# The last 64 weight rows: one load that names its source twice, in place of two half loads

## The chip, the cores and the metric

The kernel runs on one core of one Trainium2 chip. The core has TensorE (PE: matrix products; PEld: its weight loads), VectorE (DVE), ScalarE (ACT), GpSimd (POOL) and SyncE (SP, which issues DMAs and computes nothing), and 16 DMA engines that move data between HBM, the chip's main memory, and SBUF, the working memory of 128 partitions. The metric is the device time of the program in microseconds (us). For the kernel before, three runs gave 153.39 to 153.58 us with a median of 153.56 us.

## The reference

An input of 2048 tokens of width 448 is normalised over its width. The result feeds two branches, and both are added to the input:

```
xn  = layernorm(x)                                   # x: 2048 x 448
q, k, v = split(xn @ wqkv)                           # 16 heads of 28
phi(a)  = concat(softmax(a @ w_phi), softmax(-a @ w_phi))     # per head
num = phi(q) @ (phi(k)^T @ v);  den = phi(q) @ sum_s phi(k) + 1e-6
A   = (num / den) @ wo
B   = mish(xn @ w1 + b1) @ w2                        # 1792 hidden columns
out = x + A + B
```

Everything is bf16 in memory; the products are accumulated in 32 bits.

## The kernel before

**Tiles.** The 2048 tokens are 16 tiles of 128; two tiles make a unit u (8 units). The width of 448 is three chunks of 128 rows and one of 64. To use the full height of 128 rows of TensorE for the chunk of 64, the two tiles of a unit are put together: their normalised rows are transposed into seven chunks, three of each tile and one (chunk 3) whose upper half belongs to the first tile and whose lower half to the second. A product with a weight W is then run in passes: A and B cover the three full chunks in halves of 64 rows, two half products side by side, and H covers chunk 3. For H, both partition halves need the last 64 rows of W. That is why the last 64 rows (384 to 447) of the key and value weights and of W1 lie twice in SBUF: at chunk 3, in partitions 0 to 63 and again in 64 to 127.

**Loads.** A weight is loaded by two functions. `load_main` (line 275) brings rows 0 to 383 as three chunks. `load_tail` (line 279) brings the last 64 rows into both halves, with one DMA per half. It is called for the key and value weights together (`lkts`: rows of 896 numbers, 1792 bytes) and for W1 (`l1ts`: rows of 1792 numbers, 3584 bytes). Both calls are issued from SyncE.

**Order.** Each engine has one instruction stream. The streams are written out by one list of steps, ORDER (line 147); a step appends its instructions to the engines that it uses, so each engine executes its part of the list in that order. Waits between engines follow from named resources: each operation lists what it reads and writes, and `resolve` (line 89) turns this into waits on semaphores. A wait holds everything behind it on its engine.

The steps around the two tail loads, on the queues that matter:

- SyncE: x tiles 0 (`lx0.1s`), key weights (`lkms`), key and value tail (`lkts`), x tiles 8 and 9, b1, four transposing loads of the query weights (`lqT`), the transpose of unit 1 (`xt1m`), x tiles 10 and 11, W1's tail (`l1ts`), the transposes of units 3, 6, 4, 7 and 5 (`xt3m` and so on, DMA transposes at line 516), W1's main part (`l1ms`), and then transposes of the query features (line 690).
- ScalarE issues the other x tiles, w_phi in four small loads of 28 rows each (line 299), and the value weights' main part.
- TensorE at the start: 12 warm-up products of zeros (line 370), the transposes of the key weights in two halves `wtk0` and `wtk1` (line 547; the second half reads chunk 3, so it waits for the tail), the transpose of unit 0, the products of the transposed key weights with w_phi (`wmk0`, `wmk1`, line 571), the transpose of unit 2, and then key, value and query products (line 429), the first of which needs all of the folded key weights `Wpk`.
- VectorE and ScalarE take the results out of PSUM, TensorE's result memory (lines 509 and 511).

W1 is read first by `f0.0B`, the first product of the second branch. The first products that read the transposed units 3 and 6 are `k3B` and `v6Ba`.

`load_x` loads of two tiles have 128 rows of 1792 bytes, those of one tile 128 rows of 896 bytes.

Of the kernel before, what the change touches and what calls it, by code (L numbers as in the profile page):

```python
# [5 lines left out]
ACT = mybir.ActivationFunctionType  # L6
ALU = mybir.AluOpType
AX = mybir.AxisListType
FP32 = mybir.dt.float32
# [3 lines left out]
D = 448  # L13
H = 16
DH = 28
F = 1792
P = 128
# [9 lines left out]
QP = 56  # L27
# [11 lines left out]
class Program:  # L39
# [13 lines left out]
    def op(self, eng, fn, r=(), w=(), dma=False, tag="", after=()):  # L53
        o = Op()
        o.tag, o.parts = tag, None
        o.eng, o.fn, o.dma, o.needed, o.count, o.sem = eng, fn, dma, False, 0, None
        o.idx = len(self.ops[eng])
        deps = list(after)
        for res in list(r) + list(w):
            if res[0] == "ps":  # L60
                deps += [a for e, a in self.psum.get(res, {}).items() if e != eng]
        for res in r:
            if res[0] != "ps":
                deps += self.writers.get(res, [])
        for res in w:
            if res[0] != "ps":
                deps += [d for d in self.writers.get(res, []) if d.dma or dma or d.eng != eng]
                deps += [d for d in self.readers.get(res, []) if d.dma or dma or d.eng != eng]
        for res in r:
            if res[0] == "ps":  # L70
                self.psum.setdefault(res, {})[eng] = o
            else:
                self.readers.setdefault(res, []).append(o)
        for res in w:
            if res[0] == "ps":
                self.psum.setdefault(res, {})[eng] = o
            else:
                self.writers[res] = [o]
                self.readers[res] = []
        o.deps = deps  # L80
        self.ops[eng].append(o)
        self.order = getattr(self, "order", [])
        self.order.append(o)
        return o

    def dma(self, eng, fn, r=(), w=(), tag=""):
        return self.op(eng, fn, r, w, dma=True, tag=tag)
# [84 lines left out]
def _kernel(es, nc, A_x, A_wqkv, A_w_phi, A_wo, B_w1, B_b1, B_w2, out):  # L172
    def sb(name, shape, dtype):
        return es.enter_context(nc.sbuf_tensor(name, shape, dtype))
# [4 lines left out]
    ident = sb("ident", [P, P], BF16)  # L179
# [4 lines left out]
    x_all = sb("x_all", [P, NT, D], BF16)  # L184
    stats = sb("stats", [P, NT, 6], FP32)
    mv = sb("mv", [P, NT, 2], FP32)
    eps_col = sb("eps_col", [P, 1], FP32)
    mhalf = sb("mhalf", [P, 4], FP32)
    lnv = sb("lnv", [P, NT], FP32)
    rstd = sb("rstd", [P, NT], FP32)  # L190
    shift = sb("shift", [P, NT], FP32)
    NXN = 4
    xn = [sb(f"xn{i}", [P, 2 * D], BF16) for i in range(NXN)]
    xnT = sb("xnT", [P, NU, 7, P], BF16)
# [4 lines left out]
    Wkv = sb("Wkv", [P, 4, 2 * D], BF16)  # L199
    Wk, Wv = Wkv[:, :, 0:D], Wkv[:, :, D:2 * D]  # L200
    WqT = sb("WqT", [P, G, 4 * P], BF16)
    Wp = [sb(n, [P, 4, D], BF16) for n in ("Wpq", "Wpk")]
# [8 lines left out]
    v_all = v_flat[:, :].rearrange("p (u i h c) -> p u i h c", u=NU, i=2, h=H)  # L211
    EqT = sb("EqT", [P, NT, 2 * G, P], BF16)
# [14 lines left out]
    def act_flat(q):  # L227
        return actT[:, q, :, :].rearrange("p f n -> p (f n)")

    def E_of(u):  # L230
        return act_flat(1)[:, u * 4 * D:(u + 1) * 4 * D].rearrange("p (s i d) -> p s i d", s=2, i=2)
# [6 lines left out]
    def Eq_of(u):  # L238
        src = Eq0[:, :] if u % 3 == 0 else act_flat(0)[:, EQ_ROWS[u % 3] * 1024:(EQ_ROWS[u % 3] + 2) * 1024]
        return src.rearrange("p (i s c) -> p i s c", i=2, s=2)  # L240
# [2 lines left out]
    home_rows = {"Wk": [("Wk", 0), ("Wt", 0), ("Wt", 1)], "Wv": [("Wv", 0)], "Wq": [("WqT", g) for g in range(G)] + [("WqTd",)],  # L243
                 "Wp1": [("Wp", 1, h, c) for h in range(2) for c in range(2)]}

    def oT_of(u):
        t, at, _ = oT_home[u // 2]
        flat = t[:, :, :].rearrange("p c f -> p (c f)")
        return flat[:, at + (u % 2) * 7 * P:at + (u % 2 + 1) * 7 * P]
# [3 lines left out]
    def bank(b, n=1):  # L253
        return PS[:, b * TCW:(b + n) * TCW]

    def bank16(b):
        return PS.bitcast(BF16)[:, 2 * b * TCW:2 * (b + 1) * TCW]
# [5 lines left out]
    op, dma = pg.op, pg.dma  # L263

    def pb(b):
        return ("ps", b)

    HALF = ((0, 64), (64, 128))
# [8 lines left out]
            w=[(name, 0)], tag="ld" + name)  # L277

    def load_tail(eng, name, dst, src):
        for i, (lo, hi) in enumerate(HALF):  # L280
            dma(eng, lambda e, lo=lo, hi=hi: e.dma_start(dst[lo:hi, 3, :], src[384:448, :]),
                w=[("Wt", i) if name == "Wkv" else (name, 1 + i)], tag="ld" + name)

    def load_qT(g, eng):
        dma(eng, lambda e: e.dma_start_transpose(WqT[:, g, 0:D], A_wqkv[:, g * GP:g * GP + P]), w=[("WqT", g)],
# [6 lines left out]
    def rows_of(name):  # L292
        return [(name, 0), ("Wt", 0), ("Wt", 1)] if name in ("Wk", "Wv") else [(name, i) for i in range(3)]
# [87 lines left out]
    def touch(*banks):  # L381
        clock[0] += 1
        for b in banks:
            used[b] = clock[0]

    def take2(hold=True):
        free = [b for b in (0, 2, 4, 6) if b not in held]
        assert free, "no pair of banks"
        b = min(free, key=lambda b: max(used[b], used[b + 1]))
        touch(b, b + 1)  # L390
        if hold:
            held.add(b)
        return b

    def free2(b):
        held.discard(b)
        touch(b, b + 1)

    def take1():
        b = min((b for b in range(8) if b - b % 2 not in held), key=lambda b: used[b])  # L400
        touch(b)
        return b

    def pe(fn, r, w, tag, after=()):
        return op("PE", fn, r=r, w=w, tag=tag, after=after)
# [8 lines left out]
    def passes(part):  # L414
        if part == "F":
            return [(c, par, (0, P)) for par in range(2) for c in range(3)]
        x = int(part == "B")
        return [(c, r ^ x, HALF[r]) for c in ((3,) if part == "H" else range(3)) for r in range(2)]

    def pe_pass(fn, r, b, part, tag):  # L420
        o = pe(fn, r, [pb(b), pb(b + 1)], tag, after=[side[b, "A" if part == "B" else "B"]] if part in "ABH" and
               (b, "A" if part == "B" else "B") in side else [])
        side[b, "B" if part == "B" else "A"] = o

    def run(e, todo, works, first, last):
        at = {par: [n for n, x in enumerate(todo) if x[1] == par] for par in range(2)}
        for n, (c, par, k) in enumerate(todo):
            o, lhs, rhs = works[par]
            ins = e.matmul(o, lhs(c, k), rhs(c, k), start=first and n == at[par][0], stop=last and n == at[par][-1])  # L429
        return ins  # L430

    def pair_part(key, part, works, r, then):
        todo = passes(part)
        if key not in open_:
            open_[key] = [take2(), set()]
        b, done = open_[key]
        first = not done
        done.add(part)
        last = done in ({"F", "H"}, {"A", "B", "H"})
        pe_pass(lambda e: run(e, todo, works(b), first, last), r, b, part, key + part)  # L440
        if last:
            then(b)
            free2(b)
# [57 lines left out]
    def transpose7(e, b, src, cut=7):  # L501
        for c in range(7):
            to = bank16(b)[:, c * P:(c + 1) * P] if c < cut else bank16(b + 1)[:, (c - cut) * P:(c - cut + 1) * P]
            ins = e.transpose(to, src[:, c * P:(c + 1) * P], ident[:])
        return ins

    def evac(eng, dst, src, r, w, tag):
        if eng == "ACT":
            op("ACT", lambda e: e.activation(dst(), src(), ACT.Copy), r=r, w=w, tag=tag)  # L509
        else:  # L510
            op("DVE", lambda e: e.tensor_copy(dst(), src()), r=r, w=w, tag=tag)  # L511
# [80 lines left out]
    def xchunk(c, par):  # L592
        return c if c == 3 or par == 0 else 4 + c

    def tok_works(u, W):
        return lambda b: [(bank(b + par)[:, 0:D],
                           lambda c, k, par=par: xnT[k[0]:k[1], u, xchunk(c, par), :],
                           lambda c, k: W[k[0]:k[1], c, :]) for par in range(2)]

    def v_mm(u, part, eng):  # L600
        def then(b):
# [86 lines left out]
    def q_turn(t):  # L688
        u = t // 2
        dma("SP", lambda e: e.dma_start_transpose(EqT[:, t, :, :], Eq_of(u)[:, t % 2, :, :].rearrange("p s c -> p (s c)")),  # L690
            r=[("Eq", u % 3, 0), ("Eq", u % 3, 1)], w=[("EqT", t)], tag=f"eT{t}")

    def bias_T():
        b = take1()
# [169 lines left out]
    def add(name, fn, *args):  # L864
        steps[name] = lambda: fn(*args)
# [34 lines left out]
    for q in range(2):  # L900
        for part in "FABH":
            for fc in range(FC):
                add(f"f{q}.{fc}{part}", ffn1, q, fc, part)
    add("kvz", kvz)
    add("wob", last_weights)
    add("table", table)
# [73 lines left out]
```

## Time and profile before

| | us |
|---|---|
| median of three runs (lowest to highest) | 153.56 (153.39 to 153.58) |
| the profiled execution's own time | 153.96 |
| its span, first to last instruction | 152.2 |
| TensorE busy | 144.6 (95%) |
| VectorE busy | 101.1 (66%) |
| ScalarE busy | 75.7 (50%) |
| GpSimd busy | 44.3 (29%) |

The profile is of one execution. An engine's busy time is the time in which it executes something; a TensorE that is busy is not at its peak, since products overlap. "SPq" and "ACTq" mark DMA issues, which aren't counted as busy. The chain of waits is followed back from the last instruction, at each step to what released it. For a DMA issue the profile gives the size and the time from issue to landing. q1 is the queue of the DMAs that SyncE issues, q10 that of ScalarE's.

### The profile page before, as it was taken

The numbers are of one execution on the slowest core, as the hardware profiler recorded it, in microseconds if no ns is written. First come the engines' busy times: TensorE is split into PE (matmuls) and PEld (weight loads), VectorE is DVE, ScalarE is ACT, GpSimd is POOL, SyncE is SP. The second block draws the span as 40 slices with busy tenths as digits, with TensorE's granted clock in tenths as the row PEclk, the third lists the DMA queues.
The fourth block names the chain that finished last, engine by engine and source line by source line (L and its number), as shares of the span: only waits on it lengthen the run. The fifth ranks groups of instructions, "written<-read, shape, count | busy, mean of one in ns | idle before, by whom it ended". The sixth has DMA issues, their size and how long they took to land.

```text
span 152.2 us, 3611 instructions
## 1 busy us (share of the span) xinstructions
PE 144.6 (95%) x1541; PEld 76.1 (50%) x1541; DVE 101.1 (66%) x223; ACT 75.7 (50%) x90; POOL 44.3 (29%) x65
## 2 busy tenths in 40 slices
PE   3978999989999979999999999999999999999993
PEld 1454545445444574445344455554544554559552
DVE  0699989599969903599606999535995999200721
ACT  3485999995995699778997730000500400000000
POOL 3385688969999950000000000000000000000000
PEclk9999999999999999999999999999999999999999
DMA  5995964989967243994399260500035000540204
GB/s 123 288 260 147 174 143 93 131 268 262 101 137 138 76 139 73 180 197 41 60 149 321 86 65 14 119 0 0 2 65 151 30 4 0 121 121 4 87 4 151
DMA packets 40436, 17.22 MB, mean 113 GB/s; under 512 B 34020, under 2 KB 39908, under 8 KB 40420
## 3 DMA queue, kind: packets, MB, share of 16 engines
q1 hardware_dynamic: 37548, 14.46, 46.9%
q10 hardware_dynamic: 2872, 2.53, 5.6%
q8 instruction: 12, 0.20, 0.5%
q14 instruction: 4, 0.03, 0.1%
HBM read 7.02 MB, written 1.84 MB: 58 GB/s over the span
## 4 chain that ended last, share of the span: by engine, by line
PE 78%; ACT 12%; DMA 4%; DVE 3%; issue 1%; ACTq 0%
PE PS L429 38%; PE PS L828 28%; PE PS L845 7%; DMA x_all<-in_A_x_dram 4%; ACT actT L609 3%; PE PS L723 2%; PE PS L650 2%; ACT actT L682 2%; ACT v_all L509 2%; DVE Sk L627 1%; ACT Wpq L509 1%; ACT Eq L682 1%; DVE v_all L511 1%; ACT Eq L509 1%; ACT Wpk L509 1%
## 5 line engine op out<-in xcount | busy, mean ns | idle before, releaser
L703 ACT ACTIVATE actT<-PS,b1T 128x1024 bf16<-128x1024 f32 x28 | 30.2, 1112 | 33.1 <-PE PS L429 33.0
L429 PE MATMUL PS<-xnT,W 64*128 64x512 bf16 x392 | 46.2, 376 | 0.0
L828 PE MATMUL PS<-W,actT 128*128 128x448 bf16 (+1 forms) x224 | 42.7, 351 | 0.0
L828 PEld LDWEIGHTS PS<-W,actT 128*128 128x128 bf16 x224 | 21.5, 98 | 20.3 <-issue 0.7
L429 PEld LDWEIGHTS PS<-xnT,W 64*128 64x128 bf16 x392 | 18.1, 94 | 21.0 <-ACT actT L703 0.4
L793 DVE TENSOR_TENSOR x_all<-PS,x_all 128x448 bf16<-128x448 f32 (+1 forms) x16 | 9.5, 616 | 20.3 <-PE PS L845 10.3
L621 POOL TENSOR_TENSOR actT<-actT,rSk 128x896 bf16<-128x896 bf16 x12 | 20.0, 1699 | 0.0
L609 ACT ACTIVATE actT<-PS 128x896 bf16<-128x896 f32 x16 | 13.7, 950 | 3.7 <-DVE stats L466 1.8
L429 PE MATMUL PS<-Wkv,xnT 64*128 64x448 bf16 x112 | 13.6, 349 | 0.6 <-DVE v_all L511 0.6
L429 PE MATMUL PS<-Wpk,xnT 64*128 64x448 bf16 x112 | 13.3, 349 | 0.5 <-ACT Wpk L509 0.5
L429 PE MATMUL PS<-Wpq,xnT 64*128 64x448 bf16 x112 | 12.7, 350 | 0.0
L466 DVE BATCH_NORM_STATS2 stats<-x_all 128x6 f32<-128x448 bf16 x15 | 9.2, 614 | 5.2 <-DMA x_all<-in_A_x_dram 5.2
L617 DVE TENSOR_REDUCE Sk<-actT 128x32 f32<-128x896 bf16 x12 | 12.5, 1043 | 0.0
L738 DVE COPY Sq<-PS 128x16 f32<-128x16 f32 x32 | 4.0, 167 | 12.5 <-PE PS L723 12.2
L749 DVE TENSOR_TENSOR xn<-v_all,rden 128x448 bf16<-128x448 f32 x16 | 10.0, 625 | 1.3 <-DMA Wkv<-xn 0.8
L746 DVE TENSOR_TENSOR v_all<-v_all 128x464 f32<-128x464 f32 x16 | 10.3, 642 | 0.6
L742 DVE TENSOR_TENSOR v_all<-PS,Sq 128x464 f32<-128x464 f32 x16 | 10.3, 642 | 0.5
L744 DVE TENSOR_TENSOR v_all<-PS,Sq 128x464 f32<-128x464 f32 x16 | 10.1, 630 | 0.0
L429 PEld LDWEIGHTS PS<-Wkv,xnT 64*128 64x128 bf16 x112 | 5.4, 94 | 6.0 <-DVE v_all L511 1.0
L682 ACT ACTIVATE actT<-PS 128x896 bf16<-128x896 f32 x10 | 8.4, 926 | 0.0
L429 PEld LDWEIGHTS PS<-Wpk,xnT 64*128 64x128 bf16 x112 | 5.3, 94 | 5.5 <-ACT Wpk L509 0.6
L429 PEld LDWEIGHTS PS<-Wpq,xnT 64*128 64x128 bf16 x112 | 5.1, 94 | 5.4 <-ACT actT L609 0.5
(85 smaller groups left out, 137.7 us busy)
## 6 DMA issues: line engine op xcount, KB each, us to landing
W<-in_B_w_dram SPq DMA_DIRECT2D x1, 1568.0 KB, 8.0
out_dram<-x_all SPq DMA_DIRECT2D x7, 224.0 KB, 2.2
W<-in_B_w_dram SPq DMA_DIRECT2D x1, 1344.0 KB, 7.2
x_all<-in_A_x_dram ACTq DMA_DIRECT2D x5, 224.0 KB, 4.1
Wo<-in_A_wo_dram ACTq DMA_DIRECT2D x2, 336.0 KB, 3.6
x_all<-in_A_x_dram SPq DMA_DIRECT2D x2, 224.0 KB, 4.9
W<-in_B_w_dram SPq DMA_DIRECT2D x2, 224.0 KB, 4.0
Wkv<-in_A_wqkv_dram SPq DMA_DIRECT2D x1, 336.0 KB, 4.2
```

The lines of the kernel that those rows point to most:

```text
L429: ins = e.matmul(o, lhs(c, k), rhs(c, k), start=first and n == at[par][0], stop=last and n == at[par][-1])
L609: op("ACT", lambda e, s=s: e.activation(E_of(u)[:, s, :, :], two(b, D), ACT.Exp, scale=1.0 if s == 0 else -1.0), r=[pb(b), pb(b + 1)], w=[ ...
L617: op("DVE", lambda e: e.tensor_reduce(Sk[u][:, s, :], Eh(), AX.X, ALU.add), r=[("E", u, s)], w=[("Sk", u, s)], tag=f"Sk{u}.{s}")
L621: op("POOL", lambda e: e.tensor_tensor(Eh(), Eh(), ap_on(rSk[u][:, s, 0:1], [[1, 2 * H], [0, DH]]), ALU.mult), r=[("E", u, s), ("rSk", u, ...
L682: op("ACT", lambda e, s=s: e.activation(Eq_of(u)[:, :, s, :].rearrange("p i (h n) -> p i h n", n=64)[:, :, :, 0:QP], two(b, D).rearrange(" ...
L703: op("ACT", lambda e: e.activation(actT[:, q, fc, :], bank(b, 2), ACT.Mish, bias=b1T[:, fc:fc + 1]), r=[("b1T",), pb(b), pb(b + 1)], w=[(" ...
L742: op("DVE", lambda e: e.tensor_tensor(tv(t1[i]), num(0), sx(1), ALU.mult), r=[pb(b), pb(b + 1), ("Sq", i, 1)], w=[("t1", i)], tag=f"ta{t}")
L744: op("DVE", lambda e: e.tensor_tensor(tv(t2), num(1), sx(0), ALU.mult), r=[pb(b), pb(b + 1), ("Sq", i, 0)], w=[("t2",)], tag=f"tb{t}")
L746: op("DVE", lambda e: e.tensor_tensor(t1[i], t1[i], t2, ALU.add), r=[("t1", i), ("t2",)], w=[("t1", i)], tag=f"tc{t}")
L749: op("DVE", lambda e: e.tensor_tensor(o_sb[(t // 2) % 2][:, t % 2, :].rearrange("p (h d) -> p h d", d=DH), t1[i][:, :, 0:DH], ap_on(rden[i ...
L828: ins = e.matmul(bank(b)[:, 0:width(t)], act_of(fc, t), W2[:, fc, 0:width(t)], start=first and fc == 0, stop=last and fc == FC - 1)
L845: ins = e.matmul(bank(b)[:, 0:w], oT_of(u)[lo:hi, cc * P:(cc + 1) * P], Wo[lo:hi, cc, 0:w], start=first and n == at[par][0], stop=last and ...
```

## The change

The tail is loaded by one DMA. Its source is an access pattern with a leading dimension of count 2 and step 0, so that the 64 rows are named twice; its destination is chunk 3 in all 128 partitions. The resources written are the same two names, now by one DMA.

```diff
     def load_tail(eng, name, dst, src):
-        for i, (lo, hi) in enumerate(HALF):
-            dma(eng, lambda e, lo=lo, hi=hi: e.dma_start(dst[lo:hi, 3, :], src[384:448, :]),
-                w=[("Wt", i) if name == "Wkv" else (name, 1 + i)], tag="ld" + name)
+        rows = src[384:448, :]
+        twice = bass.AP(tensor=rows.tensor, offset=rows.offset, ap=[[0, 2]] + [list(d) for d in rows.ap])
+        dma(eng, lambda e: e.dma_start(dst[:, 3, :], twice), w=[("Wt", i) if name == "Wkv" else (name, 1 + i) for i in range(2)],
+            tag="lt" + name)
```

The diff also brings a small buffer, some new steps, and additional written names on the transposes of the query features. ORDER is unchanged, and it contains none of the new steps:

```diff
+    nrstd = sb("nrstd", [P, 8], FP32)
...
+    XR, XC = (15, 14, 13, 12), (11, 10, 9, 8)
...
+    def early_of(t):
+        return [(n, XR.index(t)) for n in ("xR", "xRU")] if t in XR else \
+            [("xc", XC.index(t), i, n) for i in range(2) for n in range(2 if i else 1)] if t in XC else []
...
     def q_turn(t):
...
-            r=[("Eq", u % 3, 0), ("Eq", u % 3, 1)], w=[("EqT", t)], tag=f"eT{t}")
+            r=[("Eq", u % 3, 0), ("Eq", u % 3, 1)], w=[("EqT", t)] + early_of(t), tag=f"eT{t}")
...
+    for u in range(4):
+        add(f"nr{u}", minus_rstd, u)
+        for eng, c in (("ACT", "a"), ("DVE", "d"), ("both", "b")):
+            add(f"ct{u}{c}", center_T, u, eng)
...
```

More of the change, by code (lines that the diff above doesn't have):

```diff
@@ L244, in _kernel, with flat_of, xR @@
                  "Wp1": [("Wp", 1, h, c) for h in range(2) for c in range(2)]}
+    XR, XC = (15, 14, 13, 12), (11, 10, 9, 8)
+    def flat_of(t):
+        return EqT[:, t, :, :].rearrange("p c n -> p (c n)")[:, 0:7 * P]
+    def xR(u):
+        return flat_of(XR[u]).rearrange("p (c n) -> p c n", n=P)
+    def early_of(t):
+        return [(n, XR.index(t)) for n in ("xR", "xRU")] if t in XR else \
+            [("xc", XC.index(t), i, n) for i in range(2) for n in range(2 if i else 1)] if t in XC else []
     def oT_of(u):
@@ L593, in xchunk, with tok_works, x_of, x_res @@
         return c if c == 3 or par == 0 else 4 + c
-    def tok_works(u, W):
-        return lambda b: [(bank(b + par)[:, 0:D],
-                           lambda c, k, par=par: xnT[k[0]:k[1], u, xchunk(c, par), :],
+    def tok_works(u, W, early=False):
+        def x_of(c, k, par):
+            return xR(u)[k[0]:k[1], xchunk(c, par), :] if early else xnT[k[0]:k[1], u, xchunk(c, par), :]
+        return lambda b: [(bank(b + par)[:, 0:D], lambda c, k, par=par: x_of(c, k, par),
                            lambda c, k: W[k[0]:k[1], c, :]) for par in range(2)]
+    def x_res(u, early):
+        return [("xR", u), ("xRU", u)] if early else [("xnT", u), ("xnU", u)]
@@ new lines, in center, with center_T @@
+    def center(t, eng):
+        u = t // 2
+        for n, (lo, hi, at) in enumerate([(0, D, 0)] if t % 2 == 0 else [(384, D, D), (0, 384, D + 64)]):
+            src, dst = x_all[:, t, lo:hi], flat_of(XC[u])[:, at:at + hi - lo]
+            op(eng, lambda e, src=src, dst=dst: e.tensor_scalar(dst, src, mv[:, t, 0:1], 0.0, op0=ALU.subtract, op1=ALU.add),
+               r=[("x", t), ("mean", t)], w=[("xc", u, t % 2, n), ("EqT", XC[u])], tag=f"xc{t}.{n}")
+    def center_T(u, eng):
+        r = [("xc", u, 0, 0), ("xc", u, 1, 0), ("xc", u, 1, 1), ("ident",)]
+        home = [("EqT", XR[u])]
+        if eng == "both":
+            b = take2(False)
+            pe(lambda e: transpose7(e, b, flat_of(XC[u]), 3), r, [pb(b), pb(b + 1)], f"cT{u}")
+            evac("ACT", lambda: xR(u)[:, 0:3, :].rearrange("p c n -> p (c n)"), lambda: bank16(b)[:, 0:3 * P], [pb(b)],
+                 [("xR", u)] + home, f"cTe{u}")
+            evac("DVE", lambda: xR(u)[:, 3:7, :].rearrange("p c n -> p (c n)"), lambda: bank16(b + 1)[:, 0:4 * P],
+                 [pb(b + 1)], [("xRU", u)] + home, f"cTf{u}")
+            return
+        b = take1()
+        pe(lambda e: transpose7(e, b, flat_of(XC[u])), r, [pb(b)], f"cT{u}")
+        evac(eng, lambda: flat_of(XR[u]), lambda: bank16(b)[:, 0:7 * P], [pb(b)], [("xR", u), ("xRU", u)] + home, f"cTE{u}")
@@ new lines, in minus_rstd, with sign_rstd, v_early, then @@
+    def minus_rstd(u):
+        op("DVE", lambda e: e.tensor_scalar(nrstd[:, 2 * u:2 * u + 2], rstd[:, 2 * u:2 * u + 2], -1.0, 0.0, op0=ALU.mult, op1=ALU.add),
+           r=[("rstd", 2 * u), ("rstd", 2 * u + 1)], w=[("nr", u)], tag=f"nr{u}")
+    def sign_rstd(t, s):
+        return nrstd[:, t:t + 1] if s else rstd[:, t:t + 1]
+    def v_early(u, part, eng):
+        def then(b):
+            for i in range(2):
+                t = 2 * u + i
+                dst, src = v_all[:, u, i, :, 0:DH], bank(b + i)[:, 0:D].rearrange("p (h d) -> p h d", d=DH)
+                r, w = [pb(b + i), ("rstd", t)], [("v", u)] if i else [("vh", u)]
+                if eng == "ACT":
+                    op("ACT", lambda e, dst=dst, src=src, t=t: e.mul(dst, src, rstd[:, t:t + 1]), r=r, w=w, tag=f"vs{u}.{i}")
+                else:
+                    op("DVE", lambda e, dst=dst, src=src, t=t: e.tensor_scalar(dst, src, rstd[:, t:t + 1], 0.0, op0=ALU.mult,
+                                                                               op1=ALU.add), r=r, w=w, tag=f"vs{u}.{i}")
+        pair_part(f"v{u}", part, tok_works(u, Wv, True), x_res(u, True) + rows_of("Wv"), then)
@@ new lines, in k_early, with then @@
+    def k_early(u, part):
+        def then(b):
+            for s in range(2):
+                for i in range(2):
+                    t = 2 * u + i
+                    op("ACT", lambda e, s=s, i=i, t=t: e.activation(E_of(u)[:, s, i, :], bank(b + i)[:, 0:D], ACT.Exp,
+                                                                    scale=sign_rstd(t, s)),
+                       r=[pb(b + i), ("rstd", t), ("nr", u)], w=[("E", u, s)] if i else [("Eh", u, s)], tag=f"exkc{u}.{s}.{i}")
+        pair_part(f"k{u}", part, tok_works(u, Wp[1], True),
+                  x_res(u, True) + [("Wp", 1, h, c) for h in range(2) for c in range(2)], then)
@@ new lines, in q_early, with then @@
+    def q_early(u, part):
+        def then(b):
+            for s in range(2):
+                for i in range(2):
+                    t = 2 * u + i
+                    op("ACT", lambda e, s=s, i=i, t=t: e.activation(
+                        Eq_of(u)[:, i, s, :].rearrange("p (h n) -> p h n", n=64)[:, :, 0:QP],
+                        bank(b + i)[:, 0:D].rearrange("p (h n) -> p h n", n=QP), ACT.Exp, scale=sign_rstd(t, s)),
+                       r=[pb(b + i), ("Eqp", u % 3), ("rstd", t), ("nr", u)], w=[("Eq", u % 3, s)],
+                       tag=f"exqc{u}.{s}.{i}")
+        pair_part(f"q{u}", part, tok_works(u, Wp[0], True), x_res(u, True) + [("Wp", 0, c) for c in range(4)], then)
@@ L903, in _kernel @@
                 add(f"f{q}.{fc}{part}", ffn1, q, fc, part)
+    for u in range(4):
+        add(f"nr{u}", minus_rstd, u)
+        for eng, c in (("ACT", "a"), ("DVE", "d"), ("both", "b")):
+            add(f"ct{u}{c}", center_T, u, eng)
+        for part in "ABH":
+            add(f"v{u}{part}e", v_early, u, part, "ACT")
+            add(f"v{u}{part}f", v_early, u, part, "DVE")
+            add(f"k{u}{part}c", k_early, u, part)
+            add(f"q{u}{part}c", q_early, u, part)
+        for t in (2 * u, 2 * u + 1):
+            add(f"xc{t}d", center, t, "DVE")
+            add(f"xc{t}p", center, t, "POOL")
     add("kvz", kvz)
```

## The prediction

> **What bounds the kernel now.** I read the page first (its span), then the chain of waits that ended last.
>
> ```profile
> span 152.2 us, 3611 instructions
> ```
>
> Chain of waits, in order of time (start, length, what):
>
> ```profile
> 1.74 5.48 DMA x_all<-in_A_x_dram
> ...
> 11.06 0.81 ACT Wpk L509
> ...
> 11.92 4.17 PE PS L429 x42
> ...
> 26.52 1.62 ACT Eq L682 x2
> ...
> 34.21 18.73 PE PS L429 x184
> ```
>
> The chain has no hole. Until 11.92 us it is the preparation of the key weights, until 34 us TensorE and ScalarE take turns, and from 34.21 us it is TensorE alone in long runs. So whatever holds TensorE before 34 us is paid at the end nearly in full, unless the work behind it had been waiting anyway. No tail load stands in the chain; they are hidden. The question is what covers them, and by how much. SyncE's queue:
>
> ```profile
> 1.27 0.42 SPq L276 DMA_DIRECT2D Wkv<-in_A_wqkv_dram  x1
> 1.74 1.19 SPq L281 DMA_DIRECT2D Wkv<-in_A_wqkv_dram  x2
> ...
> 16.49 1.11 SPq L281 DMA_DIRECT2D W<-in_B_w_dram  x2
> 18.98 9.90 SPq L516 DMA_TRANSPOSE xnT<-xn  x5
> ```
>
> **What the change removes.** One issue on SyncE per tail: 1.19/2 = 0.6 us at 1.7 us and 1.11/2 = 0.55 us at 16.5 us. SyncE is on the chain at neither place, so I price this at nothing; the cover is the x tiles on ScalarE's queue, which the chain waits for until 7.23 us. The new names and steps besides (nrstd, the early steps, the extra written names on the transposes of tiles 8 to 15) issue nothing in this order and meet no other reader or writer: nothing, but for 32 bytes per partition that move later buffers. Bytes stay the same: 64 rows, each landing twice.
>
> **What it adds: over how many DMA engines the load is spread.** The page has 16 of them. Does a load always use all? ScalarE's queue answers, because all its issues are listed:
>
> ```profile
> q10 hardware_dynamic: 2872, 2.53, 5.6%
> ...
> x_all<-in_A_x_dram ACTq DMA_DIRECT2D x5, 224.0 KB, 4.1
> Wo<-in_A_wo_dram ACTq DMA_DIRECT2D x2, 336.0 KB, 3.6
> ...
> Wkv<-in_A_wqkv_dram ACTq DMA_DIRECT2D x1, 336.0 KB, 3.8
> ...
> x_all<-in_A_x_dram ACTq DMA_DIRECT2D x1, 112.0 KB, 2.8
> Wo<-in_A_wo_dram ACTq DMA_DIRECT2D x2, 56.0 KB, 4.7
> ...
> out_dram<-x_all ACTq DMA_DIRECT2D x1, 96.0 KB, 1.7
> Wbd<-in_A_w_phi_dram ACTq DMA_DIRECT2D x4, 6.1 KB
> ```
>
> One packet per contiguous row: 6 x loads and one store of 128, three loads of 384, two of 64 make 2176; the four Wbd loads (28 rows of 4 pieces) make 448. Sixteen issues with sixteen reports of completion each would add 256: 2880. The page has 2872, eight fewer: two for each of the 28-row loads. So these report 14 times, not 16 (and are the ones with no time to landing). A load is dealt out by its leading count: 128 and 64 rows go to 16 engines, 28 rows to 14, the largest number up to 16 that divides 28. The new load has leading count 2 at its source (the name written twice) and 128 at its destination. The trace shows no such load; its bounds are 16 engines, if the destination's count decides, and 2, if both lists must divide. I take 2: a share must be cut at the same place in both lists, and the source list can be cut only into two.
>
> By the Trainium skill, page "DMA: Bandwidth & Descriptors", section "Rules for kernel authors", an outermost zero-step count c confines a DMA to at most c engines; the 14 reports agree with its counting rule, and the trace of before has no load with c = 2. The same section advises one 128-partition load over two half loads, which by itself would make the sum zero.
>
> **Price of two engines.** Rate of one engine, from stretches with full queues (length, then busy of PE, PEld, DVE, ACT, POOL, clock, DMA share, GB/s):
>
> ```profile
> 13.20:13.80 0.60, 0.60 (x10) 0.29 (x6) 0.60 (x3) 0.00 (x0) 0.52 (x2) 1.00 1.01 385
> 5.00:7.50 2.50, 2.50 (x13) 1.06 (x11) 1.24 (x4) 1.63 (x5) 1.20 (x3) 1.00 1.14 256
> 31.00:35.00 4.00, 3.40 (x38) 1.75 (x36) 3.97 (x4) 2.91 (x4) 2.84 (x3) 1.00 0.97 319
> ```
>
> 385/16 = 24 GB/s alone; 256/1.14/16 = 14 in the crowded start; 319/0.97/16 = 20.6 under large rows.
>
> *Key/value tail.* Each engine gets 64 x 1792 B = 114,688 B: 4.8 us at 24 GB/s, 8.2 us at 14. Landing times from issue: the load ahead (L276), then the two tails (L281):
>
> ```profile
> DMA to landing us min/median/max: 4.2/4.2/4.2
> ```
>
> ```profile
> DMA to landing us min/median/max: 5.2/5.2/5.3
> ```
>
> So before, the second half landed at 2.3 + 5.3 = 7.6 us. Now the tail begins when the load ahead is through, 1.3 + 4.2 = 5.5 us, and lands at 10.3 us if nothing shares its engines, at 13.7 us at the crowded rate. ScalarE's queue shares them:
>
> ```profile
> 6.36 0.40 ACTq L276 DMA_DIRECT2D Wkv<-in_A_wqkv_dram  x1
> 6.79 0.61 ACTq L273 DMA_DIRECT2D x_all<-in_A_x_dram  x1
> ```
>
> 336 + 224 KB over 16 engines at 24 GB/s are 1.5 us. I take T = 10.3 + 1.5 = 11.8 us. Who waits: the step wtk1, the second half of the L547 transposes, and behind it everything on TensorE, which runs in order.
>
> ```profile
> 7.17 1.17 PE L547 MATMUL PS<-ident,Wkv 128*112 128x128 bf16 x16
> ...
> 9.44 0.66 DVE L511 COPY Eq<-PS 112x1024 bf16<-112x1024 bf16 x1
> ...
> 9.90 0.96 PE L571 MATMUL PS<-Wbd,Eq 112*128 112x112 bf16 x16 [0.34 <-ACT Eq L509]
> ...
> 10.02 0.41 DVE L511 COPY xnT<-PS 128x512 bf16<-128x512 bf16 x1
> ...
> 10.50 1.09 DVE L511 CAST Wpk<-PS 128x896 bf16<-128x896 f32 x1
> ```
>
> From T: 8 transposes 0.6, then on VectorE its copy 0.66, the xnT copy 0.41 and the cast 1.09, together 2.8; the other branch (0.6 + 0.66 + 0.48 for 8 of the L571 products + 0.81 on ScalarE, as in the chain) is 2.6. With hand-overs of some 0.05 us each, 3.0. The first key product moves from 11.92 to 14.8 us: **+2.9 us** (T = 10.3 gives +1.4, T = 13.7 gives +4.8). Before, the 7.6 us landing had over a microsecond to spare, since VectorE came to the copy only at 9.44. Queued behind the tail on SyncE's ring are x tiles 8 and 9, b1 and the WqT transposes; their users stand behind this stall, so they add nothing.
>
> *W1 tail.* Its data are not needed before 38 us, but its place in the queue matters: the xnT transposes of units 3, 6, 4, 7 and 5 follow it. Each engine gets 64 x 3584 B = 229,376 B: 9.5 us at 24 GB/s, 11.1 at 20.6. Where transposes stand behind a large load is shown by W1's main load (issued 28.93 us, first fence) and the two EqT transposes behind it (issued 29.6, 30.8, second and third):
>
> ```profile
> DMA to landing us min/median/max: 7.2/7.2/7.2
> ```
>
> ```profile
> DMA to landing us min/median/max: 7.7/7.7/7.7
> ```
>
> ```profile
> L690 SPq DMA_TRANSPOSE EqT<-actT x1: 5149/5149/5149, 30.8 to 30.8; - x1
> DMA to landing us min/median/max: 7.3/7.3/7.3
> ```
>
> The load landed at 36.1, they at 37.3 and 38.1: 1.1 and 2.0 us after it, the second's issue held for 5.15 us. The W1 tail's two halves, issued from 16.49, landed so long after issue:
>
> ```profile
> DMA to landing us min/median/max: 3.8/4.0/4.1
> ```
>
> The first landed at 20.3; its 14,336 B per engine take 0.6 us, so its packets began at 19.7 at the latest. I take 19.0, 0.7 for the report of completion. With the first shift it runs from 21.9 to 31.4, and unit 3's transpose lands at 32.5, unit 6's at 33.4. Their users, keys of 3 and values of 6:
>
> ```profile
> 24.67 0.73 PE L429 MATMUL PS<-Wpk,xnT 64*128 64x448 bf16 x6
> 25.24 0.73 PE L429 MATMUL PS<-Wkv,xnT 64*128 64x448 bf16 x6
> ...
> 25.99 0.35 PE L429 MATMUL PS<-Wpq,xnT 64*128 64x448 bf16 x2
> ```
>
> Shifted, TensorE is there at 27.6 and waits 4.9 us. ScalarE is busy until 26.52 and then, for the L682 work, needs the query product at 26.0 that stands behind: a cover of 0.3. **+4.6 us**; between +2.8 (idle VectorE and TensorE time about 33 us takes some back) and +6.3 (the slower rate).
>
> **The sum** against the profiled execution's own 153.96 us (152.2 span and 1.8 around it): + 2.9 + 4.6 = 161.5. That execution is 0.4 above the median of the runs, 153.56, so on the runs' scale **161.1 us**. Its own range, from the bounds: 153.6 + 1.4 + 2.8 = 157.8 to 153.6 + 4.8 + 6.3 = 164.7.
>
> **The rivals.**
>
> *Sixteen engines, no change: 153.5 us.* The destination's 128 rows decide, the two halves' packets follow each other as now, and only covered SyncE time is saved. For it: every load with a destination of 64 or 128 rows lands normally. Against it: the 14 reports.
>
> *Sixteen engines, and faster: 153.1 us.* One issue fewer lets the tail's packets out 0.6 us sooner and off ScalarE's x loads; the chain waits on such a load until 7.23 us, with VectorE's statistics behind it, so at most that 0.6 and rather 0.4 us comes off. It decides only if the load is spread as before, and the bytes that the x load competes with stay the same, which speaks against it.
>
> *Only one stall counts: 157 us.* If the key tail lands by 9 us, VectorE's own lateness (9.44) covers it, which leaves 153.6 + 4.6 = 158; or the transposes slip past the W1 tail, which leaves 153.6 + 2.9 = 156.5.
>
> *TensorE also slows: 163.5 us.* Both stalls leave it idle for 4 to 5 us, which happens nowhere now. Its speed at the start and later:
>
> ```profile
> 2.31 5.03 PE L370 MATMUL PS<-zeros 128*128 128x512 bf16 x12 [2.31 <-POOL zeros L322]
> 46.05 2.32 PE L429 MATMUL PS<-xnT,W 64*128 64x512 bf16 x20
> ```
>
> The first 12 products of 512 columns take 0.42 us each, later ones run as pairs in 2.32/10 = 0.23. If an idle stretch brings the first speed back, the 4.17 us of products from 11.92 would double for part of it, some 2 us per stall; one such event gives 161.1 + 2.4. The trace's granted clock is 1.00 in every stretch shown, so nothing here tells how long an idle stretch must be. By the Trainium skill, page "TensorE: Matmul & The Clock Gate", section "Part 1: The HAM clock gate", about 3.4 us of idle can halve the clock; the trace of before has no such idle stretch after the warm-up.
>
> **Chances.** Two engines with both stalls 0.48; the same and a slower TensorE 0.22; one stall only 0.12; no change 0.13; faster 0.05. A difference of 0.2% (0.3 us) is about what the runs can tell from none. Slower: 0.48 + 0.22 + 0.12 = 0.82; same 0.13; faster 0.05. The range 157 to 165 holds the three slower cases but for the lowest part of the third, and leaves the 0.18 of the others out.
>
> **What would show it.** Right: the two tail issues of the changed kernel have no time to landing; a wait of 3 to 5 us before the second half of the L547 transposes; the first L429 group near 14.8 us; a wait of 4 to 5 us before the Wpk products of unit 3, with the xnT transposes issued or landed late. Wrong: tails that land about 4 to 5 us after issue as now, or L547 in one group near 7.2 us.

## The result, and the profile after

The changed kernel takes 165.16 us (median of four runs, 164.88 to 165.41), beside 153.49 us for the kernel before: 1.076 times as long, 95% interval 1.074 to 1.078, or 11.7 us more. The forecast was 161.1 us, 7.5 more. The sign, the two places and the two engines were as forecast; the size was not, and the time lies 0.16 us above the range of 157 to 165 us.

The page of the changed kernel (its span, the queue that SyncE's DMAs use, and the issues of the tails):

```profile
span 163.5 us, 3607 instructions
...
q1 hardware_dynamic: 37488, 14.46, 52.2%
...
W<-in_B_w_dram SPq DMA_DIRECT2D x1, 448.0 KB
```

The row of this queue in the page of before:

```profile
q1 hardware_dynamic: 37548, 14.46, 46.9%
```

Four half loads with 16 reports of completion each have become two loads: if all else is the same, 64 reports fewer and 2 x k more, and 60 fewer in all means k = 2. The W1 tail has no time to landing any more, as none of the other loads with fewer than 16 reports here has. So the load runs on two engines; the trace has, for each of the two tails, one report soon after the issue and two at the end (the key and value tail's at 10.99 and 11.14 us).

TensorE in order of time (start, length, what; in brackets the idle time before it and what ended it):

```profile
6.21 0.61 PE L561 MATMUL PS<-ident,Wkv 128*112 128x128 bf16 x8
11.18 0.65 PE L561 MATMUL PS<-ident,Wkv 128*112 128x128 bf16 x8 [4.37 <-DMA Wkv<-in_A_wqkv_dram]
...
14.29 1.65 PE L585 MATMUL PS<-Wbd,Eq 112*128 112x112 bf16 x16 [1.78 <-DMA Wbd<-in_A_w_phi_dram]
...
16.96 3.05 PE L443 MATMUL PS<-Wpk,xnT 64*128 64x448 bf16 x22
...
34.05 0.74 PE L443 MATMUL PS<-Wpk,xnT 64*128 64x448 bf16 x6 [3.38 <-DMA xnT<-xn]
35.38 1.05 PE L443 MATMUL PS<-Wkv,xnT 64*128 64x448 bf16 x6 [0.58 <-DMA xnT<-xn]
```

The transposes of the key weights, one group before, are split by a wait of 4.37 us for the tail. Then comes a wait that the forecast doesn't have: 1.78 us for w_phi (Wbd). The first key product starts at 16.96 us and not at 14.8. Unit 3's products come at 34.05 instead of 24.67, unit 6's at 35.38 instead of 25.24.

Stretches of the changed kernel (after the stretch its length, the busy time of PE, PEld, DVE, ACT and POOL, then the granted clock, DMA share and GB/s):

```profile
7.00:11.00 4.00, 0.00 (x0) 0.00 (x0) 1.75 (x9) 2.06 (x4) 3.24 (x7) 1.00 1.81 51
11.80:18.60 6.80, 4.99 (x42) 3.40 (x41) 3.87 (x10) 2.28 (x5) 0.38 (x2) 0.50 0.78 145
35.70:39.00 3.30, 3.30 (x22) 1.65 (x18) 3.20 (x6) 1.73 (x2) 2.99 (x3) 0.50 1.02 111
```

The same stretches of the first stall in the kernel before:

```profile
7.00:11.00 4.00, 3.01 (x44) 2.45 (x43) 3.61 (x12) 2.87 (x10) 3.13 (x7) 1.00 1.16 284
11.80:18.60 6.80, 6.68 (x76) 3.66 (x78) 6.56 (x22) 4.66 (x9) 4.25 (x11) 1.00 0.85 160
```

While the key tail is under way, the core's DMA engines move 51 GB/s, about two engines' worth at 24 each, although loads for the other engines are queued. (The DMA share can exceed 1 because the time of every open packet is counted.) After each stall the clock is 0.50 for a while. Before, it was 1.00 from 6.9 us, where the record of the clock begins, to the last matmuls.

The chain of waits now passes through these places:

```profile
3.81 10.39 DMA Wbd<-in_A_w_phi_dram
...
28.39 6.85 DMA xnT<-xn
...
35.38 28.60 PE PS L443 x270
```

### The profile page after: what moved, and what is told of

Read it like the earlier page. It is cut to its first block, busy times and chain, and to the rows that moved or that the text cites. A ratio compares the mean times of both kernels' runs of the same rounds, so it can differ in the third digit from the quotient of the medians.

```text
span 163.5 us, 3607 instructions
## 1 busy us (share of the span) xinstructions
PE 147.6 (90%) x1541; PEld 78.7 (48%) x1541; DVE 101.7 (62%) x223; ACT 76.2 (47%) x90; POOL 44.1 (27%) x65
## 4 chain that ended last, share of the span: by engine, by line
PE 78%; DMA 11%; DVE 6%; POOL 1%; issue 1%; ACTq 1%; POOLq 0%; DVEq 0%
PE PS L443 39%; PE PS L911 26%; PE PS L928 6%; DMA Wbd<-in_A_w_phi_dram 6%; DMA xnT<-xn 4%; DVE stats L480 3%; PE PS L806 2%; PE PS L733 2%; DVE mv L481 1%; PE PS L585 1%; DVE xn L506 1%; ACTq L313 1%; PE PS L518 1%; POOL rstd L489 0%; DVE x_all L876 0%
## 5 line engine op out<-in xcount | busy, mean ns | idle before, releaser
L443 PE MATMUL PS<-Wpk,xnT 64*128 64x448 bf16 x112 | 14.8, 378 | 3.4 <-DMA xnT<-xn 3.4
L443 PE MATMUL PS<-Wkv,xnT 64*128 64x448 bf16 x112 | 14.8, 371 | 0.6 <-DMA xnT<-xn 0.6
L700 DVE TENSOR_REDUCE Sk<-actT 128x32 f32<-128x896 bf16 x12 | 12.5, 1044 | 0.0
L821 DVE COPY Sq<-PS 128x16 f32<-128x16 f32 x32 | 4.0, 167 | 12.4 <-PE PS L806 12.2
L443 PEld LDWEIGHTS PS<-Wpk,xnT 64*128 64x128 bf16 x112 | 6.1, 102 | 9.4 <-issue 5.2
```

What stands on the lines that cost most here:

```text
L700: op("DVE", lambda e: e.tensor_reduce(Sk[u][:, s, :], Eh(), AX.X, ALU.add), r=[("E", u, s)], w=[("Sk", u, s)], tag=f"Sk{u}.{s}")
```

## The experiments

Each kernel is the changed one with the edit shown. "Before" is run beside each group, and differences are taken against the median of that group (153.49 for the changed kernel, then 153.99, 153.93 and 153.71 us). One more kernel, with the query weights late, has a single run and is told of in the text.

| kernel | us | ratio to before (95%) | difference, us |
|---|---|---|---|
| changed | 165.16 | 1.076 (1.074 to 1.078) | +11.7 |
| leading count 64 | 153.88 | 1.000 (0.998 to 1.002) | -0.1 |
| leading count 4 | 157.68 | 1.024 (1.019 to 1.030) | +3.7 |
| key and value tail alone | 159.63 | 1.036 (1.032 to 1.041) | +5.6 |
| W1 tail alone | 160.22 | 1.039 (1.035 to 1.043) | +6.2 |
| w_phi ahead of the tail | 164.68 | 1.070 (1.066 to 1.074) | +10.8 |
| TensorE kept busy | 165.21 | 1.072 (1.067 to 1.078) | +11.3 |
| W1 tail earlier | 167.02 | 1.085 (1.081 to 1.090) | +13.1 |
| these three together (of the fillings the first only) | 165.79 | 1.075 (1.071 to 1.080) | +11.9 |
| key tail alone, bare | 156.59 | 1.020 (1.017 to 1.023) | +2.9 |
| W1 tail alone, TensorE busy | 158.33 | 1.031 (1.028 to 1.034) | +4.6 |
| W1 tail alone, two units by TensorE | 155.31 | 1.012 (1.009 to 1.015) | +1.6 |

### Is it the number of engines, or the doubled reading?

The same load, with another dimension first. The first added line has the leading count 64, the second, in a kernel of its own, the leading count 4:

```diff
-        twice = bass.AP(..., ap=[[0, 2]] + [list(d) for d in rows.ap])
+        twice = bass.AP(..., ap=[list(rows.ap[0]), [0, 2], list(rows.ap[1])])
+        twice = bass.AP(..., ap=[[0, 4], [rows.ap[0][0], 32], list(rows.ap[1])])
```

> One load of the tail that still names each of its 64 source rows twice, but with the 64 rows as the leading count and the doubling inside (row, copy, column). The rows then lie in another order in the 128 partitions, so the products use permuted weights; bytes, packets and the one issue stay the same. Theory (a load is dealt out by its leading count, two copies at the head mean two engines): 16 engines again, both tail loads have a time to landing of 4 to 5 us, no wait before the second half of the key weights' transposes, 153.2 to 153.8 us. Rival (a load that reads the same HBM rows twice, or one load of 128 rows, is slow in itself): stays above 160 us. Rival (the new buffer and names cost something): also stays at 165 us.

> One load that names the first 32 tail rows four times (leading count 4), so that the last 32 rows aren't loaded and the weights' tail is not the reference's; bytes and packets as in the changed kernel. Theory: four engines, five reports (12 at once, then four), 32 packets each: the key and value tail lands near 9 us, the first key product comes at 12.5 to 13.5 us, W1's tail takes 4.8 us on its engines and lands about 5.5 us after the x load ahead, unit 3's products wait less than 1.5 us; 154.5 to 156.5 us. If the doubled reading itself were slow and not the number of engines, 165 us.

With 64 rows leading, the whole loss is gone: ratio 1.000 (0.998 to 1.002). Its load of the key and value tail lands as it should, and the transposes are one group again. Two rows, the first from the page's issues and the second from TensorE's timeline:

```profile
Wkv<-in_A_wqkv_dram SPq DMA_DIRECT2D x1, 224.0 KB, 5.2
...
7.24 1.06 PE L561 MATMUL PS<-ident,Wkv 128*112 128x128 bf16 x16
```

Same bytes, same single issue, same doubled reading, same added buffer and names: it is the leading count. It also answers the rival of a faster kernel. One issue fewer per tail, with the load on 16 engines, gains nothing that can be measured (the interval is 0.35 us to either side).

With a leading count of 4, the loss is a third of it. The row of SyncE's queue has 37492 packets, four more than in the changed kernel, that is two more engines for each of two loads:

```profile
q1 hardware_dynamic: 37492, 14.46, 49.1%
```

The time is 1.2 us above what I had expected. The first key product came at 13.88 us instead of 13.5 at most, since x tiles on ScalarE's queue were late as well (the last report of tiles 2 and 3 came at 9.19 us, the others by 6.1), and unit 3's products waited 0.86 us. The expectation also left out the clock: TensorE ran at half speed from 12.7 to 16.2 us, and the 22 first products took 3.36 us and not 2.25. No single wait here was long: 1.54 us, 0.65 us of work and 1.47 us.

```profile
8.82 0.65 PE L561 MATMUL PS<-ident,Wkv 128*112 128x128 bf16 x8 [1.54 <-DMA Wkv<-in_A_wqkv_dram]
10.95 0.56 PE L518 MATMUL PS<-ident,xn 128*128 128x128 bf16 x7 [1.47 <-ACT xn L509]
...
13.88 3.36 PE L443 MATMUL PS<-Wpk,xnT 64*128 64x448 bf16 x22
...
28.76 0.74 PE L443 MATMUL PS<-Wpk,xnT 64*128 64x448 bf16 x6 [0.86 <-DMA xnT<-xn]
```

The rule of the Trainium skill that the prediction weighed (page "DMA: Bandwidth & Descriptors", section "Rules for kernel authors": an outermost zero-step count c confines a DMA to at most c engines) holds here for c = 2 and 4. Its advice in the same section to use one 128-partition load in place of two half loads gave 1.000 at best.

### Each tail alone

For the other name, the two half loads of before are issued:

```diff
     def load_tail(eng, name, dst, src):
+        if name != "Wkv":            # or "W1"
...
+            return
```

> The key and value tail by one load that names its source twice, W1's tail by two half loads as before. Theory: only the first stall: tail at 11.1 us, w_phi near 14.2 us, first key product near 17.0 us (5.0 us late), another 0.8 us from half-speed TensorE, nothing at units 3 and 6: 158.5 to 159.8 us. If the stalls were not independent (the second is caused by the first), 162 us or more.

> W1's tail by one load that names its source twice, the key and value tail by two half loads as before. Theory: first key product at 11.9 us as before; W1's tail lands near 28.3 us, unit 3's transpose near 29.2 and unit 6's near 30.5; TensorE waits 4.5 us before unit 3's key products and then runs a stretch at half clock: 158.5 to 160.2 us. If unit 3's transpose doesn't wait behind the tail: 153.5 us.

Measured: +5.6 and +6.2 us, together 11.9, beside 11.7 for both at once. The two losses add up, and neither hides the other. W1's tail landed at 27.6 us by its completion reports and unit 3's products started at 28.61:

```profile
28.61 1.30 PE L448 MATMUL PS<-Wpk,xnT 64*128 64x448 bf16 x6 [3.55 <-DMA xnT<-xn]
```

The expectation was 0.02 us short for this one. A stretch at half clock follows the wait:

```profile
27.60:34.30 6.70, 5.63 (x30) 2.44 (x32) 4.90 (x10) 2.10 (x3) 4.35 (x4) 0.50 1.07 162
```

### What the forecast had left out of the first stall

The forecast had the first key product at 14.8 us; it came at 16.96, behind w_phi. I first thought that w_phi's small packets shared the two busy engines with the tail, one for one. Issued ahead of the tail on SyncE:

```diff
-... zero st1d lpa st5a st0d ...
+... zero st1d st5a st0d ...
-lkts xn4p lx8.10s ...
+lps lkts xn4p lx8.10s ...
```

> The changed kernel, with the four w_phi loads issued on SyncE ahead of the key and value tail, in place of ScalarE behind its x loads. Theory (the small w_phi packets shared the two engines with the tail, one for one, and so held the products of the key weights with w_phi from 12.4 to 14.3 us): w_phi lands by 8 us, the tail still near 11 to 12 us, the w_phi products begin near 12.4 us and the first key product near 15 us; 162.8 to 163.9 us. Rival (VectorE, not w_phi, sets the time of the first key product): 165 us, first key product at 17 us.

```profile
11.31 0.65 PE L561 MATMUL PS<-ident,Wkv 128*112 128x128 bf16 x8 [4.29 <-DMA Wkv<-in_A_wqkv_dram]
11.80 0.57 PE L518 MATMUL PS<-ident,xn 128*128 128x128 bf16 x7
12.19 1.68 PE L585 MATMUL PS<-Wbd,Eq 112*128 112x112 bf16 x16
...
14.97 2.37 PE L443 MATMUL PS<-Wpk,xnT 64*128 64x448 bf16 x20
```

No wait for w_phi, and the first key product at 14.97 us, as forecast. So w_phi is the missing step there. But the run ended at 164.68 us, above the range I had given. Of the 2.0 us gained at the start, 0.5 to 0.9 are left at the end. The second stall was followed by a longer stretch at half clock, 6.8 us instead of 3.4 (the row below lies in it), and the first by a shorter one, 3.4 instead of 6.8. That a slow stretch costs more behind the second stall, where products follow each other closely, would fit; no run shows it apart.

```profile
32.80:39.40 6.60, 5.89 (x33) 2.82 (x34) 4.13 (x8) 3.45 (x4) 5.99 (x5) 0.50 0.97 180
```

Why w_phi was late is another question, and this kernel doesn't answer it. The reports of completion in the trace speak against sharing. Those of the second w_phi load (14 engines, us):

```
changed kernel:   8.10 8.23 | 12.61 12.97 13.00 13.01 13.06 13.08 13.12 13.14 13.37 13.39 13.40 13.53
```

Two engines were done at 8.2 us, and twelve only after 12.6. The next two w_phi loads have two early reports as well, at 8.8 and 8.9 and at 9.5 and 9.6 us: two engines that work on through the stall, as the two with the tail do, and so it is the twelve without it that were late. What stood in their way? Behind the tail on SyncE's queue are the four transposing loads of the query weights. If those need all engines to go on, they would sit in the 14 free ones until the two busy ones arrive. The packets in the trace look like it: 24 packets of these transposes (256 bytes; 18 ns is the median of such a packet) began from 6.6 to 7.4 us and ended together at 12.0 to 12.1, 0.9 us after the tail. In the second stall 17 packets of the transposes behind W1's tail began from 26.0 to 26.4 us and ended at 32.8 to 32.9, where that tail landed (32.97). In the kernel with the key tail alone, packets of ScalarE's own loads were held in the same way: 14 of 896 bytes began from 7.1 to 7.9 us and ended at 12.0 to 12.2. To test the transposes, they were issued behind unit 1's transpose:

```diff
-... xt0b lqT3 rt3a wmk0d wmk1a pp b1 xt2b xn2d st8d lqT1 lqT2 lqT0 xn3d
+... xt0b rt3a wmk0d wmk1a pp b1 xt2b xn2d st8d xn3d
-... k2B xt1m st7d qd
+... k2B xt1m lqT3 lqT1 lqT2 lqT0 st7d qd
```

> The changed kernel with the four transposing loads of the query weights issued behind unit 1's transpose instead of behind the key tail; nothing else is moved, so VectorE will wait for them later and the whole time says nothing. Theory (the transposes behind the tail wait on all engines for the two busy ones, and hold the 14 free engines for whatever else is queued there): with no transpose behind the tail, x tiles 8 and 9 and w_phi land before 10 us though the tail still lands near 11 us, w_phi's products follow the tail at 12.4 us and not 14.3, first key product at 14.8 to 15.3 us. Rival (w_phi is late because its packets share the two busy engines with the tail): w_phi lands near 14 us as before, first key product at 17 us.

```
query weights late:   6.63 6.66 6.71 6.74 6.75 6.77 6.78 6.79 6.82 6.87 6.91 7.17 | 7.92 8.66
```

Now twelve engines reported by 7.2 us, and the two with the tail at 7.9 and 8.7. Fourteen of the sixteen reports of x tiles 8 and 9, queued on SyncE right behind the tail, came by 6.8 us, and the two others after it at 12.3 and 12.5. TensorE's timeline has no wait for w_phi, and the DMA engines moved three times as much in the same stretch, with the tail still under way (it landed at 11.6):

```profile
7.00:11.00 4.00, 0.72 (x10) 0.49 (x8) 1.79 (x9) 2.06 (x4) 3.10 (x6) 0.90 0.55 169
...
11.63 1.10 PE L561 MATMUL PS<-ident,Wkv 128*112 128x128 bf16 x8 [3.90 <-DMA Wkv<-in_A_wqkv_dram]
12.52 0.95 PE L518 MATMUL PS<-ident,xn 128*128 128x128 bf16 x7
13.27 1.70 PE L585 MATMUL PS<-Wbd,Eq 112*128 112x112 bf16 x16
...
15.98 1.25 PE L443 MATMUL PS<-Wpk,xnT 64*128 64x448 bf16 x6
```

The first key product came at 15.98 and not by 15.3 us: here TensorE was at half speed from 10.2 us on, before the tail landed, and the transposes of 1.10 us show it. The kernel's 168.28 us (one run) says nothing on the stall: VectorE now waits 6.8 us for the query weights.

### The clock

```diff
-... z12 wtk0a rt2a wtk1d xt0b ...
+... z12 wtk0a z16 z3 rt2a wtk1d xt0b z6 ...
-... q0A q1A q0B k3B ...
+... q0A q1A q0B z15 k3B ...
```

> The changed kernel with idle TensorE filled by products of zeros: 19 of 512 columns before the wait for the tail, 6 after the transpose of unit 0, 15 before unit 3's key products. Nothing else is moved. Theory (each idle stretch brings half speed for 3.4 to 6.8 us, worth about 0.8 us after the first stall and 1.5 us after the second): granted clock 1.00 throughout after the start, unit 3's products 0.57 us for six and not 0.8, 162.3 to 163.7 us. Rival (the slow stretches are hidden behind VectorE and ScalarE): 164.8 to 165.4 us.

In the profiled execution the clock stayed at 1.00; unit 3's products took 0.74 us, and unit 6's 0.74 and not 1.05:

```profile
6.60:40.00 33.40, 29.83 (x280) 15.78 (x280) 20.80 (x58) 19.70 (x33) 18.13 (x37) 1.00 0.94 114
...
15.96 2.25 PE L443 MATMUL PS<-Wpk,xnT 64*128 64x448 bf16 x22 [0.40 <-ACT Wpk L523]
...
34.36 0.74 PE L443 MATMUL PS<-Wpk,xnT 64*128 64x448 bf16 x6 [2.10 <-DMA xnT<-xn]
```

The first key product is 1.0 us earlier, but unit 3's products 0.3 us later: W1's tail reported at 31.9 us, 1.1 earlier than in the changed kernel, and yet the transpose behind it landed at 34.2, 2.3 us after the tail and not 0.9. Why it came so late I haven't found out. The runs (164.07 to 165.67 us) don't tell this kernel from the changed one. Their median, 165.21 us, misses the expected 162.3 to 163.7 and lies where the rival put it. But the clock of 1.00 holds for the profiled run alone, the fastest, with a span of 162.3 us, 1.2 less; the three others had a mean clock of 0.99 and took 165.03 to 165.67 us, so the filling didn't keep the clock up each time, and this kernel doesn't decide between theory and rival. The clean test of the clock is W1's tail alone, with 15 products of zeros before unit 3's:

> Only W1's tail by one load that names its source twice, with 15 products of zeros ahead of unit 3's key products to keep TensorE busy in the wait. What is left is the late transposes alone, which the prediction's second term put at +4.6 us. Theory: granted clock 1.00, unit 3's key products near 28.6 us, 157.6 to 159.0 us. If the slow stretch of TensorE costs nothing, 160.2 us as with W1's tail alone.

```profile
24.70:34.00 9.30, 8.18 (x65) 4.04 (x65) 4.91 (x10) 4.58 (x7) 4.70 (x6) 1.00 0.82 117
...
28.70 0.74 PE L448 MATMUL PS<-Wpk,xnT 64*128 64x448 bf16 x6 [0.49 <-DMA xnT<-xn]
```

Unit 3's products start at the same time as without the filling (28.70 and 28.61 us), at full clock, and the kernel takes +4.6 us instead of +6.2. The half clock after the second stall is worth about 1.6 us. Its length isn't the same in each run: of the four without the filling, the profiled one had a mean clock of 0.978 and took 160.25 us, the others 0.989, by my estimate half as long at half clock (0.011 of 158 us is lost by 3.5 us at half speed), and they took 159.39 to 160.42 us. So the 1.6 us can't be turned into a price per us.

### Other places for W1's tail

```diff
-... lqT1 lqT2 lqT0 xn3d
+... lqT1 lqT2 lqT0 l1ts xn3d
-st13d xn6d l1ts st15d ...
+st13d xn6d st15d ...
```

> The changed kernel with W1's tail issued earlier on SyncE: right behind the transposing loads of the query weights, into the pause before unit 1's transpose. Still one load on two engines, 9 to 10 us on them. Theory (the second stall is the transposes of units 3 and 6 standing behind the tail): unit 3's transpose lands before its use, no wait there and no half clock, unit 1's transpose lands up to 1 us late; 159.0 to 160.8 us. If the tail delays whatever it stands beside by the same amount, 164 us or more.

This missed. The transposing loads of the query weights ahead of it were done only at 16.2 us, so the tail lasted until 26.8 us and not 23, and the first thing behind it was unit 1's transpose, which is needed earlier than unit 3's:

```profile
29.25 1.30 PE L443 MATMUL PS<-Wpk,xnT 64*128 64x448 bf16 x6 [4.67 <-DMA xnT<-xn]
```

The stall has moved from unit 3 to unit 1 and grown, and units 3 and 6 don't wait. The three edits together (of the fillings, the 19 products before the wait for the key tail) inherit it:

> The changed kernel with w_phi ahead of the key and value tail, W1's tail issued early, and 19 products of zeros before the wait for the key tail. What is left is the late key tail alone, as the prediction's first term counted it (+2.9 us). Theory: first key product near 14.9 us, granted clock 1.00, 156.0 to 157.3 us. If the late tail costs more than its own delay, 158 us or more.

There the first key product came at 15.16 us with TensorE at full clock, as expected, and then unit 1 waited 7.21 us. The total, 165.79 us, misses the expectation for this reason and says nothing on the first term.

What the tail costs when little waits behind it is told by leaving the DMA transposes of units 3 and 6 out of its way: TensorE does them, and W1's tail is the only doubled load.

```diff
-... xn7d xt3m v0Ha ... st10d xt6m xn8p ... rt14a q1B
+... xn7d v0Ha ... st10d xn8p ... rt14a xt3b xt6b q1B
```

> Only W1's tail by one load that names its source twice; the transposes of units 3 and 6 by TensorE (and taken out by ScalarE and VectorE) instead of by DMA behind the tail. Theory (W1's late tail itself costs nothing, only what stands behind it): unit 3's key products near 25.5 us, the next DMA transpose (unit 4) lands behind the tail at about 29 us and is needed after 31 us; 154.3 to 156.5 us. Rival (the busy engines slow the core in another way): 158.5 us or more.

```profile
22.50 0.94 PE L523 MATMUL PS<-ident,xn 128*128 128x128 bf16 x14 [0.97 <-ACT actT L697]
...
26.23 0.73 PE L448 MATMUL PS<-Wpk,xnT 64*128 64x448 bf16 x6
```

+1.6 us instead of +6.2, though the tail is as late as ever (27.8 us). A wait of 0.97 us and 0.9 us of extra products on TensorE are enough to account for it. So nothing is left that the late W1 rows themselves would cost.

### The prediction's two terms, each alone

The second term is the run above with W1's tail and TensorE kept busy: +4.6 us. For the first, only the key and value tail is doubled, w_phi goes ahead of it, and 19 products of zeros fill the wait:

> Only the key and value tail by one load that names its source twice (W1's by two halves), w_phi issued ahead of it, and 19 products of zeros keep TensorE busy in the wait. What is left is the late key tail alone, which the prediction's first term put at +2.9 us. Theory: first key product near 15 us, granted clock 1.00, 156.2 to 157.4 us. If the first term itself was too small, 158.5 us or more.

```profile
7.60:16.00 8.40, 7.91 (x73) 4.60 (x72) 4.74 (x14) 4.04 (x9) 3.11 (x7) 1.00 1.15 130
...
14.87 1.48 PE L448 MATMUL PS<-Wpk,xnT 64*128 64x448 bf16 x13 [0.49 <-ACT Wpk L528]
```

First key product at 14.87 us, and +2.9 us in the runs. What these additions (w_phi moved, the products of zeros) do to the kernel before was not measured, so both terms hold only as far as the additions themselves cost nothing.

## Why the prediction was right and wrong

**Right.** Two engines (60 packets fewer, and the kernels with leading counts 64 and 4). The key tail landed at 11.1 us by its reports, forecast 11.8. In the kernel with the key tail alone, bare, it landed at 11.7 us and the first key product came 3.2 us later, at 14.87 (forecast 3.0 later, at 14.8). W1's tail lasted about 9 us behind the x load ahead of it (forecast 9.5), and unit 3's transpose landed 0.9 us after it, forecast 1.1. Measured alone, the terms are +2.9 us (forecast +2.9) and +4.6 us (forecast +4.6). That the second agrees to 0.1 us is in part luck: unit 3's products came only 4.0 us late there (24.67 to 28.70), and a further wait of 0.63 us for unit 6's transpose, which the sum doesn't have, made up the rest.

**Wrong: the sum of 7.5 us left out two costs that the same stalls bring.** Of the measured 11.7 us, 4.2 were missing; taken as differences between kernels, the two costs come to 4.4.

| | us |
|---|---|
| late key tail alone | +2.9 |
| w_phi held, and half clock, in the first stall (5.6 - 2.9) | +2.8 |
| late transposes of units 3 and 6 alone | +4.6 |
| half clock in the second stall (6.2 - 4.6) | +1.6 |
| sum | +11.9 |
| measured, both tails | +11.7 |

The first step that failed is the sentence that x tiles 8 and 9, b1 and the WqT transposes, queued behind the tail, "add nothing". I asked only when their own users need them. The transposing loads held the 14 free engines for ScalarE's queue too, and with them w_phi, whose products (L571 before, L585 after) stand between the tail and the first key product. The sum lets these products follow the transposes of the key weights at once; they had to wait for w_phi, 1.78 us longer.

The second is a choice: full speed of TensorE as the likeliest case, and the slow one as a rival with 0.22. Both stalls left it idle for 3.4 to 4.4 us in one piece, and both were followed by half clock, 6.8 and 3.4 us long. That rival was right in kind, and its price of some 2 us per stall was near 1.6 for the second; the total was set at one event (163.5 us) instead of two. What the Trainium skill says there (page "TensorE: Matmul & The Clock Gate", section "Part 1: The HAM clock gate", half speed after about 3.4 us of idle) agrees with these stretches; as both waits were forecast above 3.4 us, it should have had the larger chance. It isn't the whole rule here: with the leading count 4, half clock followed two waits of 1.54 and 1.47 us with 0.65 us of work between them.

How the 2.8 us of the first stall divide depends on the order. At the first key product, w_phi ahead of the tail brings 1.1 us at full clock (15.96 to 14.87) and 2.0 at half (16.96 to 14.97); keeping TensorE busy brings 1.0 while w_phi is late (16.96 to 15.96) and 0.1 when it is not (14.97 to 14.87).

**The rivals.** No change and faster with sixteen engines: the kernel with leading count 64 shows what they would have looked like, 1.000, and the 0.4 us of the faster one lies just outside the interval. Only one stall: each stall alone costs 5.6 and 6.2 us.

## What to carry to other kernels

Put the dimension with the many rows first in a DMA's access pattern: a count of 2 at the head puts the whole transfer on two engines, and its price here was set by what is queued behind it, above all by DMA transposes. With the 64 rows first, the copies land in another order of partitions, which the products would have to follow; here that gained nothing over two half loads. When waits for TensorE are forecast at some microseconds in all, even with a little work between them, price the slow clock after them in the sum, and not beside it. And when a queue is held, ask for every load on the other queue too, not only for those behind it.

## What was not expected of the hardware

- In this kernel, DMA transposes that stood behind a load on two engines held the other 14 for both queues until that load was done. DMA traffic fell to 51 GB/s from 7 to 11 us, where the kernel without transposes there moved 169; twelve engines reported w_phi's second load at 12.6 to 13.5 us instead of 6.6 to 7.2.
- The half-clock stretches in the traces last 3.4 us, twice or three times that: 6.8 and 3.4 us in the changed kernel, 3.4 and 6.8 with w_phi ahead of the tail, 10.2 around the first stall with W1's tail earlier. What decides the length isn't shown. Half clock can also follow waits of only 1.5 us, as with the leading count 4.
- One issue less on SyncE is worth nothing here, with the load spread as before: 1.000, 0.998 to 1.002.
